# Score visits of three chunks, unit 2 normed on VectorE, and the first pair loaded by head, in a fused cosine attention and cosine-gated MLP

## The chip, the cores and the metric

The kernel runs on one core of a Trainium2 chip. The metric is the device time of one execution in microseconds (us), as the median of five runs. Beside it stands one profiled execution, whose trace gives the times of all instructions. Engines are named as in the profile: PE (TensorE), PEld (its weight loads), DVE (VectorE), ACT (ScalarE), POOL (GpSimd) and SP (SyncE, which here only issues transfers).

## The reference

Attention over 8 batches, 12 heads, 448 positions and 64 channels, with q and k normed to length 1, and then an MLP on the joined heads (3584 rows of 768):

```
q_n = q / (norm(q) + 1e-6);  k_n = k / (norm(k) + 1e-6)
attn = softmax(q_n @ k_n.T / tau)            # tau = 0.1
x = (attn @ v), heads side by side           # 3584 x 768
h = x @ w_in                                 # 768 x 2048
out = (h * cos(h)) @ w_out                   # 2048 x 768
```

Inputs and output are float32.

## The kernel before

**Units and pairs.** A batch has 12 heads: two units of six heads, each of three pairs. Pairs are numbered g = 0 to 47, units u = 0 to 15; batch b holds pairs 6b to 6b + 5. A sequence of 448 is laid out as 112 partitions by 4.

**What a pair needs.** `load` brings k and q of a pair or of a whole unit into `raw` (two buffers, by the parity of u), `load_v` brings v. The norm of a pair is a chain: `square` (on ACT, DVE or POOL, by `PLAN` for units 0 and 1, mostly POOL afterwards), `reduce` (a DVE reduction), `rnorm` (ACT: logarithm, then exponential of minus a half of it, L708 and L711; one call for a whole unit from unit 2 on) and `scale` (POOL, or DVE for pair 0). `transposes` turns the scaled pair into `qkT`: by PE and a DVE copy (L745, L753) for g < `BYPE` = 9, by a DMA transpose issued from SP afterwards (L734). `copy_v` casts v into `va`.

**Scores and attention.** A pair's scores come in four chunks of 112 keys. `scores` makes a chunk for two heads at once, each in one half of PE's rows (L762), in bank SC1 or SC0 by turns, and an ACT exponential takes it out into `PX` (L767). `both` makes two chunks back to back: this document calls such a run of score matmuls a visit. `attend` multiplies a pair's `PX` with `va` into bank AV (32 small matmuls, L785), and DVE takes the reciprocal of the sums and the product (`rcp` L794, `xs` L795). `xs` is transposed into `xT`, by PE (`XP`, in bank AV, L809, for batch 0 and the last pair of each batch) or by a DMA transpose from SP (L801).

**The MLP.** `m1(b)` is the first product for a batch: 16 column blocks of six matmuls of 448 columns (96 in all, L826), two blocks to a bank, over three banks by turns (`TURN`: SC0, SC1, AV), each followed by ACT's sine with a shift (L840) and a DVE product into `gT` (L842). M1's blocks 0 to 7 use the first half of W1, 8 to 15 the second. The second product, M2, makes 128 rows by 384 columns in 16 matmuls (L877) into PO or PO2, and a DVE copy into `osb` (L884); outputs are issued from SP. M2 is the filling work: PE takes it while ACT makes exponentials.

**Tables.** ACT loads a table before the sines and another before the exponentials (1.28 us each, L618).

**The order.** The program is a list of operations with their dependences. A planner in the kernel (`arrange`, `play`, `rehearse`) plays the list with constants for the costs, several times with other margins (`TRIALS`), keeps one order for each engine, and `emit` writes it out with semaphore waits, so each engine's order is fixed when the kernel runs. PE's main stream is taken nearly in program order, M2 (stream B) wherever it fits; where the plan has holes, matmuls of zeros are put in (the fillers, L919). The order of POOL and SP matters because both also issue transfers: W1 (L908) and W2 (L914) are issued from POOL and cast on the way, all else from SP, but for the first unit's q, from ACT.

**Around the change.** The first six pairs are computed while the weights come in; `norms(2, 0)` stands before `m1(0)`, so ACT makes unit 2's logarithms before it loads the sine table. `pair(g)` is the body of the main loop: two visits, `attend(g - 1)` between them, loads and norms for later units. `points` puts `m1(b)` after pair 12 for b = 1 and after one pair more of the next batch for the others, and all of M2 of that batch is queued behind it.

Of the kernel before, what the change touches and what calls it, by code (L numbers as in the profile page):

```python
# [6 lines left out]
ACT = mybir.ActivationFunctionType  # L7
# [7 lines left out]
    "sq": ["AD", "A", "P", "P", "P", "P"],  # L15
# [4 lines left out]
DEBUG = 0  # L20
PACE, AHEAD = 0.97, 9.5
# [7 lines left out]
class Program:  # L29
# [11 lines left out]
    PATIENCE = 0.25  # L41
# [56 lines left out]
    def share(self, start, jobs, factor=1.0, first=1.2):  # L98
# [3 lines left out]
        came = {o.idx: start[o.idx] + first + (0.5 if e == "POOL" else -0.1) for e in jobs for o in jobs[e]}  # L102
# [69 lines left out]
    TRIALS = [(m, h, k) for m in ((0.0, 1.0), (0.3, 1.1), (0.8, 1.1)) for h in (0.1, 0.2) for k in (0.05, 0.2)]  # L172
# [3 lines left out]
    def arrange(self):  # L176
# [12 lines left out]
        for self.margin, self.hold, self.look in self.TRIALS:  # L189
            nominal, self.lands = first, {}  # L190
            for n in range(self.PASSES):
# [14 lines left out]
                if n:  # L206
                    spans = [self.rehearse(f, x) for f, x in self.STAGE]
                    if DEBUG:
                        print(self.margin, self.hold, self.look, n, "%.1f" % self.span, ["%.1f" % x for x in spans])
# [8 lines left out]
    def play(self):  # L218
# [45 lines left out]
        def pick():  # L264
# [4 lines left out]
            if groups and groups[0][0].free:  # L269
                for grp in groups[: self.WINDOW]:  # L270
# [3 lines left out]
                    if left[o.idx] == 0:  # L274
                        t = max(free["PE"], ready_at[o.idx])
                        if s is None or t < s - self.PATIENCE:
                            s, c = t, (t, o, grp)
                return c
            for grp in groups[:3]:
                t = when(grp)  # L280
                if t is not None and (s is None or switched(t, grp[0]) < s - self.PATIENCE):
                    s, c = switched(t, grp[0]), (t, grp[0], grp)
            if fill and left[fill[0].idx] == 0:
                o = fill[0]
                t = max(free["PE"], ready_at[o.idx])
# [16 lines left out]
        def transfer(upto):  # L302

            while clock[0] < upto:
# [10 lines left out]
                for h in run:  # L315
                    h[2] -= step * h[0].pkt / turn
                    if h[2] <= 1e-9:
                        o = queue[h[0].eng].pop(0)[0]
                        o.end = max(clock[0] + self.LAST, o.start + o.cost + 1.0)
                        if o.start > 5.0:  # L320
                            o.end += self.margin[0] + (self.margin[1] - 1.0) * (o.end - o.start)
# [8 lines left out]
        while todo or any(queue.values()):  # L330
# [23 lines left out]
            if e == "PE":  # L354
                if current:
                    current.pop(0)
                elif grp is fill:
                    fill.pop(0)
# [15 lines left out]
            if o.dma is not None:  # L374
                queue[e].append([o, o.start + (1.7 if e == "POOL" else 1.1), o.bulk + 0.02])
# [110 lines left out]
def bass_cosine_attention__then__act_gcu_kernel(  # L486
# [25 lines left out]
    BYPE = 9  # L512
# [5 lines left out]
    NO = 4  # L518
    DEFER = (2 * PB,)
# [58 lines left out]
    POv = PO.ap().bitcast(BF16)  # L578
    vav = [t.ap().rearrange("p (x d) -> p x d", d=DV) for t in va]
# [9 lines left out]
    XTv = AV.ap().bitcast(BF16)  # L589
# [48 lines left out]
    for i in range(2):  # L638
        pool(lambda e, i=i: e.memset(vav[i][:, :, D : D + 1], 1.0), (), [("va", i)], 0.15, label="ones")
# [7 lines left out]
    def load(u, p0, p1, apart=False):  # L647
        i = u % 2
        h = slice(2 * p0, 2 * p1)
        f = [lambda e, x=x, t=t: e.dma_start(  # L650
            rawv[i][:, h, NJ * x : NJ * x + NJ, :].rearrange("p h s d -> p h (s d)"), src(t, u, 2 * p0, 2 * (p1 - p0)))
            for x, t in enumerate((k, q))]
        for x in ((0,), (1,)) if apart else ((0, 1),):
            eng = "ACT" if u in HALF and x == (1,) else "SP"
            behind = quick[-1] if eng == "ACT" and quick else None if eng == "ACT" or not loads else loads[-1]
            dma(eng, [f[y] for y in x], (), [("raw", i, p, y) for p in range(p0, p1) for y in x],
                "raw%d_%d_%s%s" % (i, p0, x, eng), 0.95 * (p1 - p0) * len(x), "load u%d p%d" % (u, p0), behind, 0.068)
# [421 lines left out]
```

## Time and profile before

| | us |
|---|---|
| median of five runs | 433.33 (431.95 to 433.84) |
| the profiled execution | 431.95 |
| its span | 430.1 |
| PE busy, of the span | 418.3 |
| ACT busy | 264.5 |
| DVE busy | 212.7 |
| POOL busy | 192.9 |
| ACT exponentials (L767), 192 of 914 ns | 165.0 |
| M2 matmuls (L877) into PO, 816 | 148.6 |
| fillers (L919), 48 | 14.5 |

The span is the time from the first to the last instruction in the trace. "Busy" of PE counts the fillers, and the ends of matmuls are modelled, so the distance from one start to the next is the better measure of what a matmul costs. The last M1 starts near 377 us and 200 M2 matmuls follow it. The DMA engines are at or near 90% in the first 65 us, and moved 234 to 266 GB/s there. The granted TensorE clock is full throughout.

### The profile page before, as it was taken

What the parts mean: (1) busy time and instruction counts of PE and PEld (TensorE: products, weight loads), DVE (VectorE), ACT (ScalarE), POOL (GpSimd) and SP (SyncE); (2) the same over time, 40 slices, a digit from 0 to 9 for tenths busy, and PEclk for the clock granted to TensorE, in tenths of its full rate; (3) what the DMA queues carried; (4) which work ended last, traced back from release to release, by engine and by line L of the source; (5) the groups of instructions that cost most, each with busy time, mean ns of one, the idle gap of its engine ahead of it and who ended that gap; (6) DMA issues with size and microseconds to landing.
All of it is one profiled execution on the core that took longest, in us unless ns stands there. A gap on an engine that the chain in (4) does not pass through costs nothing.

```text
span 430.1 us, 8767 instructions
## 1 busy us (share of the span) xinstructions
PE 418.3 (97%) x3756; PEld 226.1 (53%) x3756; DVE 212.7 (49%) x297; ACT 264.5 (61%) x319; POOL 192.9 (45%) x118
## 2 busy tenths in 40 slices
PE   7889989999999999999999999999999999999996
PEld 3455545545555555555555545555555545555663
DVE  5776645464636366524853375425853343344221
ACT  3887386974777647774677638774777557734000
POOL 3995167823776556923496057913595000000000
PEclk9999999999999999999999999999999999999999
DMA  8999997898179595649657694649657102200322
GB/s 234 263 244 215 241 266 164 146 265 195 34 194 227 129 276 163 121 102 252 171 113 124 152 243 103 112 128 251 145 112 125 49 0 59 59 2 4 102 77 77
DMA packets 94631, 63.87 MB, mean 149 GB/s; under 512 B 55040, under 2 KB 89600, under 8 KB 94592
## 3 DMA queue, kind: packets, MB, share of 16 engines
q1 hardware_dynamic: 90064, 56.16, 56.0%
q0 software_dynamic: 3680, 6.29, 7.9%
q10 hardware_dynamic: 848, 0.86, 0.7%
q8 instruction: 30, 0.49, 0.5%
q14 instruction: 9, 0.07, 0.1%
HBM read 45.61 MB, written 11.01 MB: 132 GB/s over the span
## 4 chain that ended last, share of the span: by engine, by line
PE 82%; ACT 7%; POOL 3%; issue 2%; DVE 2%; DMA 2%; SPq 1%; POOLq 0%; ACTq 0%
PE PO L877 28%; PE SC L826 20%; PE AV L826 11%; PE AV L785 10%; PE SC L762 9%; ACT PX L767 5%; PE SC L877 2%; DMA raw<-in_q_dram 2%; POOL sq L693 2%; POOL qks L719 1%; PE AV L877 1%; DVE n L700 1%; DVE gT L842 1%; ACT cosb L840 0%; PE PO L745 0%
## 5 line engine op out<-in xcount | busy, mean ns | idle before, releaser
L767 ACT ACTIVATE PX<-SC 112x896 bf16<-112x896 f32 x192 | 165.0, 914 | 43.5 <-PE SC L762 43.1
L877 PE MATMUL PO<-W,gT 128*128 128x384 bf16 x816 | 148.6, 326 | 0.0
L693 POOL TENSOR_TENSOR sq<-raw 112x1024 bf16<-112x1024 f32 x42 | 79.4, 1908 | 97.9 <-DMA raw<-in_q_dram 97.9
L877 PEld LDWEIGHTS PO<-W,gT 128*128 128x128 bf16 x816 | 73.0, 97 | 56.8 <-issue 13.1
L719 POOL TENSOR_TENSOR qks<-raw,rn 112x1024 bf16<-112x1024 f32 x47 | 88.5, 1904 | 27.9 <-ACT rn L711 27.8
L826 PE MATMUL SC<-xT,W 128*128 128x448 bf16 x480 | 95.5, 352 | 0.2 <-DVE xT L813 0.2
L842 DVE TENSOR_TENSOR gT<-SC,cosb 128x896 bf16<-128x896 f32 x40 | 43.5, 1091 | 55.2 <-ACT cosb L840 54.8
L840 ACT ACTIVATE cosb<-SC,cst 128x896 f32<-128x896 f32 x40 | 40.2, 1007 | 48.6 <-PE SC L826 46.2
L826 PEld LDWEIGHTS SC<-xT,W 128*128 128x128 bf16 x480 | 46.6, 98 | 43.0 <-issue 0.6
L700 DVE TENSOR_REDUCE n<-sq 112x16 f32<-112x1024 bf16 (+1 forms) x49 | 58.0, 1190 | 13.0 <-POOL sq L693 8.2
L762 PE MATMUL SC<-qkT 64*128 64x448 bf16 x384 | 55.5, 355 | 4.2 <-ACT PX L767 2.2
L826 PE MATMUL AV<-xT,W 128*128 128x448 bf16 x288 | 58.7, 352 | 0.6
L785 PEld LDWEIGHTS AV<-va,PX 112*128 112x128 bf16 x1536 | 49.4, 97 | 15.6 <-issue 11.3
L785 PE MATMUL AV<-va,PX 112*128 112x65 bf16 x1536 | 54.8, 193 | 1.0 <-ACT PX L767 1.0
L884 DVE COPY osb<-PO 128x384 f32<-128x384 f32 x51 | 28.2, 553 | 39.3 <-PE PO L877 39.3
L840 ACT ACTIVATE cosb<-AV,cst 128x896 f32<-128x896 f32 x24 | 24.2, 1007 | 32.0 <-PE AV L826 31.9
L794 DVE RECIPROCAL rcp<-AV 112x8 f32<-112x8 f32 x48 | 9.9, 207 | 67.0 <-PE AV L785 67.0
L826 PEld LDWEIGHTS AV<-xT,W 128*128 128x128 bf16 x288 | 27.6, 98 | 28.1 <-issue 3.1
L842 DVE TENSOR_TENSOR gT<-AV,cosb 128x896 bf16<-128x896 f32 x24 | 26.2, 1090 | 18.7 <-ACT cosb L840 18.5
L795 DVE TENSOR_TENSOR xs<-AV,rcp 112x512 bf16<-112x512 f32 x48 | 33.2, 691 | 2.0
L762 PEld LDWEIGHTS SC<-qkT 64*128 64x128 bf16 x384 | 13.3, 94 | 36.7 <-ACT PX L767 17.4
L667 POOL CAST va<-vin 112x1536 bf16<-112x1536 f32 x14 | 20.5, 1466 | 10.1 <-DVE gT L842 5.8
(34 smaller groups left out, 122.9 us busy)
## 6 DMA issues: line engine op xcount, KB each, us to landing
vin<-in_v_dram SPq DMA_DIRECT2D x16, 672.0 KB, 10.2
raw<-in_k_dram SPq DMA_DIRECT2D x12, 672.0 KB, 8.1
raw<-in_q_dram SPq DMA_DIRECT2D x12, 672.0 KB, 10.0
W<-in_moe_w_in_dram POOLq DMA_DIRECT2D x2, 1536.0 KB, 14.4
W<-in_moe_w_out_dram POOLq DMA_DIRECT2D x4, 768.0 KB, 20.9
raw<-in_k_dram SPq DMA_DIRECT2D x12, 224.0 KB, 7.0
out_dram<-osb SPq DMA_DIRECT2D x7, 336.0 KB, 2.8
out_dram<-osb SPq DMA_DIRECT2D x8, 288.0 KB, 2.7
```

The lines of the kernel that those rows point to most:

```text
L693: pool(lambda e, x=x, y=y: e.tensor_tensor(y, x, x, ALU.mult), src_, dst, 0.1 + n * 1.78e-3, label="sq%d.%d" % (u, p))
L700: dve(lambda e, w=w: e.tensor_reduce(out=n2v[i][:, 2 * p : 2 * p + 2, w], in_=sqv[p][:, :, w, :], axis=mybir.AxisListType.X, op=ALU.add), ...
L719: f = lambda e, s0=s0, s1=s1: e.tensor_tensor(qksv[i][:, p, s0:s1, :, :].rearrange("p s h d -> p h s d"), rawv[i][:, h, s0:s1, :], bass.AP ...
L762: t = e.matmul(SCv[z][:, a, 0:S], qkT[k].ap()[r, NP * c : NP * c + 128], qkT[k].ap()[r, S : 2 * S], start=True, stop=True)
L767: act(lambda e: e.activation(PXv[j][:, c, 0 : 2 * S].rearrange("p (a s) -> p a s", a=2), SCv[z][0:NP, :, 0:S], ACT.Exp, scale=1.0 / TAU), ...
L785: t = e.matmul(AVv[:, a, DV * x : DV * x + n], PXv[j][:, c, k : k + 128], vav[i][:, NJ * (2 * p + a) + c, 0:n], start=(c == 0), stop=(c == ...
L795: dve(lambda e: e.tensor_tensor(xsv[y].rearrange("p x h d -> p h x d"), AXv[:, :, :, 0:D], bass.AP(rcp[y], 0, [[NS, NP], [NJ, 2], [1, NJ], ...
L826: t = e.matmul(ph[:, a, 0:S], W1v[:, c, 128 * n : 128 * n + 128], xTv[b % 2][:, c, :], start=(c == 0), stop=(c == NKC - 1))
L840: act(lambda e, ph=ph, cz=cz: e.activation(cosv[cz], ph[:, :, 0:S], ACT.Sin, bias=cst.ap()[:, 0:1], scale=1.0), names(gi) + ["cst0"], [("c ...
L842: dve(lambda e, ph=ph, cz=cz, gi=gi: e.tensor_tensor(gTv[:, 2 * gi : 2 * gi + 2, S * (b % 2) : S * (b % 2) + S], ph[:, :, 0:S], cosv[cz], ...
L877: r = e.matmul(po[:, 0:HW], gTv[:, y, col : col + 128], W2v[:, y, HW * hf : HW * hf + HW], start=(y == 0), stop=(y == NF - 1))
L884: dve(lambda e, po=po, o=o, hf=hf: e.tensor_copy(osb[o].ap()[:, HW * hf : HW * hf + HW], po[:, 0:HW]), keys, [("osb", o, hf)], HW, label=" ...
```

## The change

1. **Visits of three.** For g >= `G3` = 12, `visit` makes three chunks, which take the banks AV, SC0, SC1; the 12 chunks of three pairs make four visits (`ahead`, `visit`, `attend`, `values`, with `project` for M1 after the second visit). Pairs 6 to 11 keep visits of two. XP and, for pairs 8 to 11, the PE transposes change banks.
2. **Unit 2.** Its loads wait until the first half of W1 has landed; its norm is done pair by pair, on DVE, by an integer guess and three Newton steps: 11 small operations for each pair. All its squares are POOL's. `BYPE` is 12: pairs 9 to 11 are transposed by PE as well.
3. **The first pair** is loaded, squared and reduced a head at a time.
4. **W1 and W2.** Both halves of W1 are issued from POOL one after the other behind the first POOL square (u0 p2); W2 is issued behind the last scale of unit 1. Unit 1's first square moves from POOL to ACT.
5. **M2** is dealt out evenly (`SPREAD`, `KEEP`): 144 matmuls of it are left after the last M1.
6. **v** is cast in thirds on DVE for units 0 and 1, and `attend` is split finer in the first six pairs. **Planner:** other margins, a larger delay for transfers from POOL, and other rules for choosing M2.

```
-    "sq": ["AD", "A", "P", "P", "P", "P"],
+    "sq": ["AD", "A", "P", "A", "P", "P"],
...
-    TRIALS = [(m, h, k) for m in ((0.0, 1.0), (0.3, 1.1), (0.8, 1.1)) for h in (0.1, 0.2) for k in (0.05, 0.2)]
+    TRIALS = [(m, h, k, p) for m in ((0.3, 1.1), (0.7, 1.1)) for h in (0.2, 0.32) for k in (0.4, 0.5) for p in (0.15, 0.25)]
...
-                queue[e].append([o, o.start + (1.7 if e == "POOL" else 1.1), o.bulk + 0.02])
+                queue[e].append([o, o.start + (5.0 if e == "POOL" else 1.1), o.bulk + 0.02])
...
-    BYPE = 9
+    BYPE = 12
...
+        if u == 0 and p0 == 0 and BYHEAD:
+            for a in range(2):
+                for x, t in enumerate((k, q)):
+                    eng, past = ("SP", loads) if x == 0 else ("ACT", quick)
+                    dma(eng, [lambda e, x=x, t=t, a=a: e.dma_start(
+                        rawv[i][:, a : a + 1, NJ * x : NJ * x + NJ, :].rearrange("p h s d -> p h (s d)"), src(t, u, a, 1))],
+                        (), [("raw", i, 0, x, a)], "raw%s%d" % (eng, a), 0.45, "load u0 p0", past[-1] if past else None, 0.063)
+                    past.append(P.ops[-1])
+            return
...
+        if u in NEWTON:
+            m, t, y = n2[i].ap()[:, w], lnn[i].ap()[:, w], rn[i].ap()[:, w]
...
+            def small(f, reads, writes):
+                dve(f, reads, writes, n, label="rn%d.%d" % (u, p0))
+
+            small(lambda e: e.tensor_scalar(m, m, 1e-12, None, ALU.add), km, km)
+            small(lambda e: e.tensor_scalar(y.bitcast(I32), m.bitcast(I32), -0.5, 1597463007.0, ALU.mult, ALU.add), km, ky)
+            for x in range(STEPS):
+                small(lambda e: e.scalar_tensor_tensor(t, y, -0.5, m, ALU.mult, ALU.mult), km + ky, kt)
+                small(lambda e: e.tensor_tensor(t, t, y, ALU.mult), kt + ky, kt)
+                small(lambda e: e.scalar_tensor_tensor(y, t, 1.5, y, ALU.add, ALU.mult), kt + ky, ky)
+            return
...
+        if g >= PB + UP - 1:
+            views, keys = (AVt, AVt), ("AV", "AV")
...
     def scores(g, c):
-        j, k, z = g % 2, g % UH, (c + 1) % 2
+        j, k, q = g % 2, g % UH, NJ * g + c
+        name, bank = PHs[1 + (c + 1) % 2 if g < G3 else q % 3]
...
+        keys, view = ["PO"], POv
+        if g >= 2 * PB - 1:
+            keys, view = [(["PO"], POv), ([("TP", 0), ("TP", 1)], TPv)][nhalf[0] % 2]
+            nhalf[0] += 1
...
+        if g >= 2 * PB - 1:
+            m2_emit(max(0, len(m2_queue) - KEEP[g // PB - 1]))
...
+    def visit(g, n):
+        q = NJ * g + 3 * n
+        for x in range(q, q + 3):
+            scores(x // NJ, x % NJ)
...
+    def project(b, g):
+        first = len(P.ops)
+        m1(b)
...
+        m2_add(b)
+        m2_emit(SPREAD[b])
...
     load_w1(0)
-    after(P.ops[-1], find("load v u0"))
     load_w1(1)
...
+    P.order_only(find("sq0.2"), find("W1.0"))
+    P.order_only(find(BEHIND), find("W1.1"))
+    last_scale = find(LASTW)
     for p in range(UP):
         load(2, p, p + 1)
+        if BEFORE2:
+            after(P.ops[-1], find(BEFORE2))
     load_w2(0)
+    P.order_only(last_scale, P.ops[-1])
     load_w2(1)
-    norms(2, 0)
...
     m1(0, 2, NKC - 1)
     copy_v(2)
     P.free = False
     banks[0] = [("PO", PO.ap()), ("PO2", PO2.ap())]
+    for p in range(UP):
+        norms(2, p, p + 1)
+        if p < UP - 1:
+            transposes(PB + p)
     m2_add(0)
...
+    m2_emit(SPREAD[0])
+    for g in range(PB, G3):
+        ahead(g)
+        grouped(both, g, 0)
+        if g > PB:
+            attend(g - 1)
...
+    for g in range(G3, NG, 3):
+        for n in range(4):
+            if n < 3:
+                ahead(g + n)
+            grouped(visit, g, n)
+            if n < 3 and g + n > PB:
+                attend(g + n - 1)
+            if n == 0:
+                values(g)
+            if g % PB == 0 and g > PB and n == (AT if g > 2 * PB else AT1):
+                project(g // PB - 1, g)
     attend(NG - 1)
```

## The prediction

> **What bounds the kernel now.** I read the shares per slice first, then the table by stage, then the timeline of one steady pair and of the first microseconds, and last the waits of the head.
>
> ```profile
> 9.50:36.50 27.00, 23.46 (x323) 12.94 (x324) 20.51 (x29) 22.92 (x35) 24.44 (x17) 1.00 1.12 248
> 36.50:58.00 21.50, 21.39 (x136) 11.40 (x135) 11.79 (x15) 10.06 (x12) 7.56 (x5) 1.00 1.14 244
> 58.00:90.00 32.00, 30.61 (x344) 16.52 (x341) 17.49 (x27) 26.84 (x35) 23.72 (x14) 1.00 0.88 184
> 239.28:287.04 47.76, 47.66 (x441) 25.55 (x440) 24.79 (x34) 32.13 (x39) 25.32 (x14) 1.00 0.71 153
> ```
>
> Columns: the stretch, its length, busy us of PE, weight load, DVE, ACT and POOL, then clock, DMA share and GB/s. From about 140 us on, PE has no idle time (47.66 of 47.76 us for one batch) while ACT has 15 us spare and DVE 23. In the head PE's 23.46 is swollen by idle fillers (48 in all); there ACT (22.92 of 27) and POOL (24.44 of 27) are nearly full, and the DMA engines are. So a steady gain must take time off PE itself; a gain in the head must shorten the ACT and POOL chain.
>
> ```profile
> 143.36 4.54 PE SC L826 x24
> 394.17 11.70 PE PO L877 x72
> ```
>
> These pieces of the chain of waits give PE's pitch: 4.54/24 = 0.189 us for 448 columns, 11.70/72 = 0.1625 for 384.
>
> ```profile
> 115.90 0.55 PE L762 MATMUL SC<-qkT 64*128 64x448 bf16 x4
> 116.30 1.73 ACT L767 ACTIVATE PX<-SC 112x896 bf16<-112x896 f32 x2 [0.69 <-PE SC L762]
> 116.38 1.14 PE L785 MATMUL AV<-va,PX 112*128 112x65 bf16 x32
> 117.36 0.81 PE L877 MATMUL PO<-W,gT 128*128 128x384 bf16 x4
> 117.56 0.21 DVE L794 RECIPROCAL rcp<-AV 112x8 f32<-112x8 f32 x1 [3.35 <-PE AV L785]
> 117.80 0.69 DVE L795 TENSOR_TENSOR xs<-AV,rcp 112x512 bf16<-112x512 f32 x1
> 118.11 0.55 PE L762 MATMUL SC<-qkT 64*128 64x448 bf16 x4
> ```
>
> One score visit, in starts: two chunks (two row halves at once) from 115.90 to 116.38 take 0.48, of which 2 x 0.189 is work: 0.10 is lost on leaving. Four M2 matmuls take 117.36 to 118.11, 0.75 for 0.65 of work: 0.10 lost on entering. A visit costs 0.20 us beside its work. Within it the second chunk starts 0.20 after the first (a narrower look at the same visit), 0.01 over the pitch.
>
> **Part 1: three chunks to a visit, from pair 12 on.** 36 pairs make 72 visits now and 48 after: 24 x 0.20 = 4.8 saved, less 24 more chunk-to-chunk steps of 0.01: **-4.6 us**. Bounds: -5.0, and -3.6 if a third chunk drains as much as a quarter of a switch. All of it is on the path, since PE is never idle there.
>
> The price is the third bank. AV now also takes a score chunk, so attend waits for that chunk's exp, and the next visit waits for xs. By the rows: exp begins 0.40 after the visit (115.90 to 116.30) and its first chunk takes 0.92, so AV is free at 1.32; the order gives PE 3 x 0.189 + 0.10 + four M2 (0.65), 1.32 with switches: no margin. Attend to xs done is 118.49 - 116.38 = 2.11; the order gives 0.96 + eight M2 (1.30) + 0.10 = 2.36: margin 0.25, if DVE is free. An osb copy (0.55) or a norm reduction (1.22) standing ahead of rcp breaks it. DVE's order puts the osb copies behind xs mostly, and two reductions in the stretch with no attend. Between 0 and 0.2 us for each of 36 attends, 0 to 7 in all; the nearer row is the margin of 0.25 that still holds with DVE half idle, so I take 0.04 each: **+1.5**.
>
> **Part 2: the head.** The first pair is loaded a head at a time, so each reduction starts when its half is there. Now q's square runs at 4.63, two reductions 5.36 to 6.65, rn at 7.26; split, the first head is reduced before the second lands, and about 0.65 (one reduction) comes off the first exp. That gain is caught at pair 1: both W1 issues (1.02 and 0.88) now stand on POOL ahead of the scales of pairs 1 and 2, where one stood; 0.9 later on POOL, against 0.65 earlier before it. In return POOL loses a square (1.9, given to ACT at 1.04) and the W2 issues that stood ahead of the last scale (1.5): 3.4 earlier by the last pair.
>
> ```profile
> POOL sq L693 <- DMA raw<-in_q_dram: 6.5, 1, 6.5
> ACT PX L767 <- PE SC L762: 5.0, 5, 1.7
> ```
>
> ACT sat 5.0 us in five waits for scores; 1.53 of them (before pair 1) stay, of the 1.8 after 23 us I count most back, less ACT's extra square. M1 of batch 0 starts at 36.34 now, **35.5** after (bounds 33.8, if only the 1.53 and the extra square are left of the 5.0, to 36.8, if W1's second half, now beside the unit-1 loads in a DMA system at 1.12 share, delays those).
>
> Unit 2's loads now wait on SP for W1's first half; behind them wait unit 3's loads, V, outputs and transposes. In the trace W issues land after 11.9 to 25.4 us. That moves unit 2's squares from 30 to about 36 us, under M1, where POOL has 12 idle us.
>
> **Part 3: unit 2's norms on DVE.** ln, rn (0.58) and a square (1.08) leave ACT ahead of the sine table. Eleven tiny operations for each of three pairs come to DVE. No such row exists; xs costs 0.69 for 512 elements and a 1024 reduction 1.21, so the constant is about 0.15, and 16 elements make 0.17, plus 0.04 between dependent operations (rcp ends 117.77, xs starts 117.80): 33 x 0.21 = 7.0 us. The bounds are the 0.06 us memset row (3.3 with gaps) and rcp's 0.21 (8.2).
>
> [...]
>
> DVE under M1 then holds 8 x 1.09 (gT) + 3 x 1.22 + 7.0 = 19.4 us against PE's 96 x 0.189 = 18.2, and eleven of them stand ahead of the last two gT. M1 has only three banks, so PE waits.
>
> ```profile
> 7.26 1.29 DVE L719 TENSOR_TENSOR qks<-raw,rn 112x512 bf16<-112x512 f32 x2 [0.62 <-ACT rn L711]
> 7.91 2.40 POOL L693 TENSOR_TENSOR sq<-raw 112x1024 bf16<-112x1024 f32 x1 [6.46 <-DMA raw<-in_q_dram]
> ```
>
> A POOL square that began beside a DVE multiply of two SBUF inputs took 2.40 instead of 1.90. So 27 of the 33 operations may in turn wait out a POOL operation (1.9 us): while pair 6 is scaled, pair 7's chain stands, then pair 8's. By the row that is up to 0.7 + 1.9 = 2.6 more.
>
> [...]
>
> The stall of PE in M1 is between 0 and 1.2 + 2.6 = 3.8; I take 2.0. M1 ends at 35.5 + 18.2 + 2.0 = 55.7, against 56.25 now (with three transposes in it that now follow).
>
> **From there to M1 of batch 1** the work is 96 M2 (15.6), 30 chunks (5.7), 7 attends (6.7), six transposes (6 x 0.39 = 2.3; three of them took the DMA path), one more 0.2, 14 visits' worth of switches (2.8): 33.3. Now 26.9 of work and 3.0 of switches take 33.9, so 4.0 are stalls, most of them the wait at 58.7 to 61.9 for first exps. Transposes and M2 fill part of that; pair 6's copy now stands behind late gT copies. I take 1.5 (0.5 to 4). M1 of batch 1 starts at 90.5, against 90.14, with two chunks, an attend and a visit (1.5) more done: **-1.1**.
>
> **Covered.** The V copies in thirds (6 x 0.69 against 2 x 1.74) lie in DVE's idle 6 us of the head. M2 moved from the tail (200 matmuls after the last M1, now 144) is the same PE work; its cover is lost only if attention were ACT-bound, and ACT has 32 of 48 us. The changed planner constants only move the order counted here.
>
> **Sum.** -1.1 - 4.6 + 1.5 = -4.2: span 430.1 to 425.9. The profiled execution took 431.95, 1.85 over its span, and the median 433.33 is 1.38 over that: 425.9 + 1.85 + 1.38 = **429.1**.
>
> **Rivals.**
> (a) The AV bank takes it back. Decides from (4.2 + 1.5)/36 = 0.16 us for each attend. If one attend in four meets a reduction of 1.22, that is 11.0: 430.1 - 1.1 - 4.6 + 11.0 = 435.4, time **438.6**, slower. For: no margin by the rows. Against: DVE half idle.
> (b) The Newton chains cost their bounds: 1.8 more in M1, 2.5 more behind: 425.9 + 4.3 = 430.2, time **433.4**, no change. For: the 2.40 us square. Against: POOL waits for the same chain, so they can't collide for long.
> (c) The early part goes well: start at 33.8, no stall in M1, 0.5 behind, no AV waits: -1.7 - 2.0 - 1.0 - 1.5 = -6.2: time **422.9**. For: 4 idle ACT us. Against: pair 1's scale is later.
> (d) The visits don't do what they say: the third chunk drains like a new visit, saving nothing: 429.1 + 4.6 = **433.7**. Against: the 0.01 step.
>
> **Chances.** Forecast 0.48, (a) 0.13, (b) 0.14, (c) 0.21, (d) 0.04. Own range of the forecast 426.5 to 431.8; to hold 8 in 10, from 424 (half of (c)) to 433.6 (most of (b); (a) is left out). A measurement tells 0.3%, 1.3 us, from no change: faster than 432.0 holds the forecast, (c) and a third of (b): 0.74; same 0.11; slower, (a) and the rest: 0.15.
>
> **What would show it.** Score rows of six matmuls, steady batches near 48.8 us at 112 M2 matmuls (now 47.76 at 100); PE waiting for xs or an AV exp by under 0.1 a pair; DVE rows of 0.17; M1 of batch 1 near 90. Wrong if steady PE idle time passes 1 us a batch, or that start lies past 93.

## The result and the profile after

| | before | after |
|---|---|---|
| median, us | 433.61 (431.85 to 437.87, 45 runs) | 434.49 (433.13 to 437.16, 24 runs) |
| profiled execution, us | 431.95 | 436.41 |
| its span, us | 430.1 | 434.6 |
| M1 of batch 0 starts at | 36.34 | 37.30 |
| M1 of batch 1 starts at | 90.14 | 94.43 |

The changed kernel is slightly slower: ratio 1.0022, 95% interval 1.0007 to 1.0037. Forecast was 429.1 with a span of 425.9. The two profiled executions lie on different sides of their medians (before 1.7 below, after 1.9 above), so their spans differ by 4.5 us where the medians differ by 0.9. The table by stage of the kernel after, with the columns of the one shown of before:

```profile
9.50:36.50 27.00, 23.20 (x292) 13.49 (x290) 17.66 (x30) 23.18 (x36) 19.81 (x14) 0.94 1.12 231
12.00:15.00 3.00, 0.58 (x4) 0.19 (x3) 2.82 (x4) 1.89 (x4) 2.99 (x3) 1.00 1.13 262
15.00:20.00 5.00, 4.58 (x56) 3.29 (x56) 2.68 (x5) 3.74 (x7) 4.48 (x4) 0.66 1.13 240
36.50:58.00 21.50, 19.95 (x142) 10.87 (x139) 18.62 (x42) 7.63 (x9) 9.48 (x5) 1.00 1.13 243
58.00:90.00 32.00, 29.92 (x355) 16.91 (x354) 19.93 (x34) 26.80 (x34) 24.74 (x14) 1.00 0.71 154
245.45:294.97 49.52, 49.34 (x457) 26.91 (x454) 24.89 (x34) 31.83 (x39) 25.34 (x14) 1.00 0.64 148
```

Three things differ. In the head PE did 0.58 us of work in 12 to 15 us, and after that its granted clock (third number from the right) was 0.66 over 5 us. In M1 of batch 0 DVE is busy 18.62 of 21.50 us (11.79 before), and PE has 1.55 us of idle time in it, where it had 0.1 before (busy 19.95 against 21.39). A stretch in which PE stands and waits is called a hole below. And a steady batch takes 49.52 us: it holds 112 M2 matmuls where the batch of before, 47.76, held 100. Twelve matmuls at 0.1625 are 1.95, so before would take 49.71 for the same work. The gain is 0.19 us a batch; 0.8 had been expected from four visits fewer at 0.20.

The pitches did not change. The chain of waits of the kernel after has

```profile
196.06 4.56 PE SC L883 x24
...
407.81 7.80 PE PO L931 x48
```

0.190 us and 0.1625 us a matmul. With them PE's lost time of a stage is its length less its matmuls at their pitch; for a steady batch it was 2.86 before (12 visits) and is 2.67 after (8 visits).

**Where the 0.8 went.** The timeline after, over two visits of three and the attends behind them, only the lines that matter (`...` stands for lines left out):

```profile
228.08 0.36 PE L811 MATMUL AV<-qkT 64*128 64x448 bf16 x2
...
228.48 0.92 ACT L816 ACTIVATE PX<-AV 112x896 bf16<-112x896 f32 x1 [0.72 <-PE AV L811]
...
228.75 0.82 PE L931 MATMUL PO<-W,gT 128*128 128x384 bf16 x4
...
229.45 1.02 PEld L834 LDWEIGHTS AV<-va,PX 112*128 112x128 bf16 x32 [0.27 <-ACT PX L816]
...
230.43 1.47 PE L931 MATMUL PO<-W,gT 128*128 128x384 bf16 x8
...
231.83 0.36 PE L811 MATMUL AV<-qkT 64*128 64x448 bf16 x2
...
232.50 1.47 PE L931 MATMUL PO<-W,gT 128*128 128x384 bf16 x8
...
233.05 1.72 ACT L816 ACTIVATE PX<-SC 112x896 bf16<-112x896 f32 x2
234.01 1.02 PEld L834 LDWEIGHTS AV<-va,PX 112*128 112x128 bf16 x32 [0.42 <-ACT PX L816]
```

A visit of three costs what was forecast: 228.08 to 228.75 is 0.67 for 0.57 of work. But attend now starts where an exponential ends. Four M2 matmuls from 228.75 are done at 229.40, attend starts at 229.45, as the exponential of the chunk in AV ends (228.48 + 0.92). The next attend needs the second chunk of its visit too, in SC0. Eight M2 from 232.50 are done at 233.80, attend starts at 234.01. A steady batch has four waits of 0.05 and two of 0.21, 0.62 in all, 0.10 for each attend. The xs product never made PE wait by more than 0.1 there.

**The head.** The chain of waits, then ACT and PE in the same stretch:

```profile
2.16 7.59 DMA raw<-in_q_dram
...
9.89 0.98 POOL sq L720
...
11.73 1.85 POOL W L964 x2
...
13.58 1.93 POOL qks L761
```

```profile
9.30 0.92 ACT L816 ACTIVATE PX<-SC 112x896 bf16<-112x896 f32 x1 [0.49 <-PE SC L811]
...
13.07 0.31 ACT L750 ACTIVATE lnn<-n,cst 112x16 f32<-112x16 f32 x1 [2.41 <-DVE n L726]
...
13.54 2.51 ACT L816 ACTIVATE PX<-SC 112x896 bf16<-112x896 f32 x3
```

```profile
10.57 1.50 PE L975 MATMUL PO<-zt 128*128 128x448 bf16 x7
14.49 0.36 PE L811 MATMUL SC<-qkT 64*128 64x448 bf16 x2 [2.42 <-ACT PX L816]
...
15.56 0.81 PE L793 MATMUL PO<-ident,qks 112*128 112x112 bf16 x8 [0.41 <-POOL qks L761]
16.16 1.53 PE L834 MATMUL AV<-va,PX 112*128 112x65 bf16 x24
```

The first exponential comes 0.57 earlier than before (9.30 against 9.87), near the 0.65 forecast, but not in the way that was forecast: the second half of q had landed at 4.24, before the first reduction began at 4.61, so no head was reduced ahead of the other's landing. And pair 2's q load, now the fourth on ACT's queue and not the third, lands at 9.75; before, POOL's square of pair 2 began at 7.91. Pair 2's logarithm stands on ACT ahead of pair 0's last three exponentials and waits 2.41 us for that square's sum; PE waits 2.42. The transposes that followed took 0.81 us for eight, where before they took 0.57: that is the clock, which by the table in stretches of half a microsecond stood at 0.50 from 15.7 to 19.1.

**M1 of batch 0.** DVE and POOL:

```profile
48.88 1.02 DVE L747 TENSOR_TENSOR lnn<-lnn,rn 112x16 f32<-112x16 f32 x1
...
51.24 0.88 DVE L747 TENSOR_TENSOR lnn<-lnn,rn 112x16 f32<-112x16 f32 x1
...
53.88 1.08 DVE L899 TENSOR_TENSOR gT<-AV,cosb 128x896 bf16<-128x896 f32 x1
...
55.58 1.89 DVE L747 TENSOR_TENSOR lnn<-lnn,rn 112x16 f32<-112x16 f32 x1
```

```profile
47.98 1.89 POOL L720 TENSOR_TENSOR sq<-raw 112x1024 bf16<-112x1024 f32 x1 [2.90 <-DMA raw<-in_q_dram]
50.19 1.90 POOL L761 TENSOR_TENSOR qks<-raw,rn 112x1024 bf16<-112x1024 f32 x1 [0.32 <-DVE lnn L746]
55.54 1.90 POOL L761 TENSOR_TENSOR qks<-raw,rn 112x1024 bf16<-112x1024 f32 x1 [3.44 <-DVE lnn L746]
```

```profile
55.10 2.43 PE L883 MATMUL AV<-xT,W 128*128 128x448 bf16 x12 [1.55 <-DVE lnn L746]
...
60.31 0.57 PE L793 MATMUL PO<-ident,qks 112*128 112x112 bf16 x8 [1.73 <-DVE qkT L801]
```

A Newton operation takes 0.17, but three that began beside a POOL operation ended with it: 48.88 + 1.02 is 49.90, the square ended at 49.87; 51.24 + 0.88 and 50.19 + 1.90 are 52.12 and 52.09; 55.58 + 1.89 and 55.54 + 1.90 are 57.47 and 57.44. Unit 2's squares wait for loads held back behind W1 until 38.20, 43.18 and 47.98. So the chains stand on DVE ahead of the gT product that frees bank AV (53.88), and PE waits 1.55 for it, then 1.73 for pair 6's copy.

### The profile page after: what moved, and what is told of

It is laid out like the page before. It is cut to its first block, busy times and chain, and to the rows that moved or that the text cites. A ratio compares the mean times of both kernels' runs of the same rounds, so it can differ in the third digit from the quotient of the medians.

```text
span 434.6 us, 8854 instructions
## 1 busy us (share of the span) xinstructions
PE 418.4 (96%) x3775; PEld 229.7 (53%) x3775; DVE 222.5 (51%) x338; ACT 262.3 (60%) x318; POOL 192.3 (44%) x118
## 4 chain that ended last, share of the span: by engine, by line
PE 73%; POOL 8%; DMA 6%; ACT 5%; DVE 3%; SPq 3%; issue 1%; ACTq 0%; POOLq 0%
PE PO L931 26%; PE SC L883 17%; PE AV L883 10%; PE AV L834 9%; POOL qks L761 5%; PE SC L811 5%; DMA raw<-in_q_dram 4%; ACT PX L816 4%; PE AV L811 3%; SPq L780 2%; POOL sq L720 2%; DMA vin<-in_v_dram 2%; PE AV L931 1%; PE SC L931 1%; DVE lnn L747 1%
## 5 line engine op out<-in xcount | busy, mean ns | idle before, releaser
L931 PE MATMUL PO<-W,gT 128*128 128x384 bf16 x832 | 152.2, 327 | 0.7 <-DVE osb L940 0.7
L816 ACT ACTIVATE PX<-SC 112x896 bf16<-112x896 f32 x144 | 122.8, 918 | 5.9 <-PE SC L811 5.9
L931 PEld LDWEIGHTS PO<-W,gT 128*128 128x128 bf16 x832 | 74.2, 98 | 64.1 <-issue 20.1
L816 ACT ACTIVATE PX<-AV 112x896 bf16<-112x896 f32 x48 | 44.0, 917 | 47.9 <-PE AV L811 47.9
L834 PEld LDWEIGHTS AV<-va,PX 112*128 112x128 bf16 x1536 | 50.4, 98 | 14.9 <-ACT PX L816 11.7
L834 PE MATMUL AV<-va,PX 112*128 112x65 bf16 x1536 | 56.8, 194 | 0.6
L811 PE MATMUL SC<-qkT 64*128 64x448 bf16 x288 | 42.1, 354 | 3.9 <-ACT PX L816 2.8
```

The source lines that it names most:

```text
L811: t = e.matmul(bank[:, a, 0:S], qkT[k].ap()[r, NP * c : NP * c + 128], qkT[k].ap()[r, S : 2 * S], start=True, stop=True)
L816: act(lambda e: e.activation(PXv[j][:, c, 0 : 2 * S].rearrange("p (a s) -> p a s", a=2), bank[0:NP, :, 0:S], ACT.Exp, scale=1.0 / TAU), [n ...
L834: t = e.matmul(AVv[:, a, DV * x : DV * x + n], PXv[j][:, c, k : k + 128], vav[i][:, NJ * (2 * p + a) + c, 0:n], start=(c == 0), stop=(c == ...
L931: r = e.matmul(po[:, 0:HW], gTv[:, y, col : col + 128], W2v[:, y, HW * hf : HW * hf + HW], start=(y == 0), stop=(y == NF - 1))
```

## The experiments

Theory A: the visits' saving is real, and attend's wait for the exponential in AV gives most of it back; the rest of the loss comes from the head (loads by head) and from DVE's order in and behind M1 of batch 0. Rivals: the visits save nothing; W1's two issues on POOL make the head late; the chains' operations themselves, not their place, make the holes; the planner's constants do it. The last one has one test only (`soon0`, one constant); no run puts the other constants back.

**Both kernels again, and visits of two.** `c_before` is the kernel before unchanged, `c_after` the changed one. `two` keeps all of the change but the visits of three (with it, M1 of a batch stands after a whole pair again, and other numbers of M2 matmuls fall into a batch):

```
-    G3 = 12
+    G3 = NG
...
-    for g in range(PB, G3):
+    for g in range(PB, NG):
```

> The kernel before, unchanged, for a second profile of it. If the two profiles of before and after were ordinary ones, this one has its M1 of batch 0 start within 1 us of 36.3, M1 of batch 1 near 90.1 and steady batches of 47.76. If the head varies from run to run (its transfers fill the DMA engines), the start of M1 of batch 0 moves by 1 us or more, and part of the 4.5 us between the two profiled spans is no effect of the change.

> The changed kernel, unchanged. Ratio to before about 1.002. Theory 'head varies': M1 of batch 0 starts anywhere in 35 to 37.5 and the span shifts with it, while the steady batches stay at 49.53 with 112 M2 matmuls. Theory 'the change delays the head': M1 of batch 0 starts at 37.3 again and POOL's first square at 9.9.

> The changed kernel with visits of two chunks for all pairs, nothing else undone. Theory A (the 24 visits fewer save 0.20 us each, but attend now waits 0.05 to 0.21 us for the exponential of a chunk of its own visit, 0.6 us a batch): a steady batch of 112 M2 goes from 49.53 to 49.7, the whole by 1 us or less. My prediction's term (saving 4.6, waits 1.5) would make it 3 us slower than the changed kernel. Rival (three banks cost more than they bring): up to 2 us faster.

`c_before` took 435.86 (one run, span 434.0): its M1 of batch 1 started at 91.45, and PE had a hole of 1.46 at 161.4 to 162.8 that the first profile had not. So these two executions of the kernel before differ by 3.9 us of span, and such a hole is in one and not in the other. `c_after` took 435.85, ratio 1.0029 (1.0004 to 1.0054), with steady batches of 49.52 to 49.53 again. `two` took 438.07, ratio 1.0104 (1.0059 to 1.0149), 2.2 us above `c_after`. Its undisturbed steady batch (116 M2) lost 2.68, as much as with visits of three; one hole of 2.03 at 142.6, for a DMA transpose of xs, shows in it. What makes it slower over its runs is not settled by its one profile, so `two` alone does not show what the visits are worth.

**Half an exponential in AV.** From pair 24 on `halfexp` leaves out half of each exponential in bank AV, so its output is not the reference's; it is there to time the wait.

```
+        ha = 1 if name == "AV" and g >= 2 * G3 else 2
-        act(lambda e: e.activation(PXv[j][:, c, 0 : 2 * S]..., bank[0:NP, :, 0:S],
+        act(lambda e: e.activation(PXv[j][:, c, 0 : ha * S]..., bank[0:NP, 0:ha, 0:S],
```

> The changed kernel, same order on every engine, but from pair 24 on the exponential of each chunk that lies in bank AV takes one head of the two (448 columns instead of 896); the other head's part of PX keeps older values, so half of these chunks is left out. Theory V (attend waits for the exponential that empties bank AV, 0.62 us a steady batch of the changed kernel, as two waits of 0.21 and four of 0.05): that exponential ends 0.4 earlier, the four waits of 0.05 and one part of the two of 0.21 go, a steady batch at 112 M2 matmuls takes 48.9 to 49.1 instead of 49.53, PE's lost time per batch 2.1 to 2.3 instead of 2.67, the whole kernel 2 to 3 us (0.5 to 0.7%) below the changed kernel. Rival S (the third chunk of a visit or the new order costs PE itself, not the wait for the exponential): the batch stays at 49.5.

The table by stage of this kernel (one steady batch), and one cycle of its timeline:

```profile
242.88:291.76 48.88, 48.78 (x458) 27.40 (x455) 24.90 (x34) 28.85 (x39) 25.34 (x14) 1.00 0.62 150
```

```profile
226.30 0.54 ACT L817 ACTIVATE PX<-AV 112x448 bf16<-112x448 f32 x1 [1.04 <-PE AV L811]
...
226.57 0.82 PE L932 MATMUL PO<-W,gT 128*128 128x384 bf16 x4
...
227.23 1.13 PE L835 MATMUL AV<-va,PX 112*128 112x65 bf16 x32
```

With the same order, attend follows its four M2 at once (226.57 + 0.65 is 227.22), a batch takes 48.88 and PE loses 2.02 in it: 0.84 less than before. Median 432.41, ratio 0.9952 (0.9929 to 0.9976), against 1.0022 for the changed kernel. 0.84 is the forecast saving of the visits; with the longer exponential 0.65 of it is taken back in each batch.

**The head.** `nohead` loads the first pair whole (`BYHEAD = False`), `w1late` puts W1's second half behind pair 1's scale (`P.order_only(find("scale1.0"), find("W1.1"))`), `soon0` sets `SOON = 0.0`.

> The changed kernel with its first pair loaded whole, as in the kernel before (part 3 of the change undone); everything else stays. Theory H (the head starts late because each pair-0 load is cut in four and the loads behind them, those of pair 2 and of q above all, land later, so that POOL's first square waits to 9.89 instead of 7.91, and everything on POOL behind it): that square again near 8, pair 1's first exponential near 16.5 instead of 18.2, M1 of batch 0 near 36.0 instead of 37.3, ratio to the kernel before 0.3% lower than that of the changed kernel (1.0022): about 0.999. Rival W (the late head comes from the two W1 issues that stand on POOL ahead of pair 1's scale, not from the loads): the first square may move but pair 1's scale stays near 13 and M1 of batch 0 near 37, ratio 1.002.

> The changed kernel with W1's second half issued from POOL behind the scale of pair 1 instead of behind the first square; everything else stays. Rival W: pair 1's scale begins 0.9 to 1.0 us earlier (12.6 instead of 13.6), its first exponential near 17.2, M1 of batch 0 near 36.4, ratio to the kernel before about 1.000. Theory H: the first square still waits for its load to 9.9, POOL then has the same work a little later, ACT's row of exponentials is only shifted, M1 of batch 0 within 0.3 of 37.3 and the ratio near 1.002.

> The changed kernel with the one planner constant that pulls the logarithms of the first two units forward (SOON) set from -4 to 0: on ACT the exponentials of pair 0's chunks now stand ahead of pair 2's logarithm. Nothing is left out. Theory A (in the changed kernel pair 2's logarithm, which waits for POOL's late square, stands ahead of pair 0's last three exponentials; ACT stalls 2.41 us, PE 2.42, and PE's granted clock then falls to 0.66 in 15 to 20 us): no PE hole over 1 us before 16 us, clock 1.00 in 15 to 20 us, M1 of batch 0 starts at 36.0 to 36.5 instead of 37.3, ratio to the kernel before 0.999. Rival L (the hole is POOL's and the loads', the order on ACT only decides where it is seen): the hole appears before pair 1's scores instead, M1 of batch 0 at 37 or later, ratio 1.002.

| | first POOL square | pair 1's scale | PE hole before 16.2 us | half clock | M1 of batch 0 | ratio |
|---|---|---|---|---|---|---|
| after | 9.89 | 13.58 | 2.42 | 15.7 to 19.1 | 37.30 | 1.0022 |
| nohead | 8.68 | 12.39 | 0.29 | none | 35.52 | 0.9981 (0.9956 to 1.0007) |
| w1late | 9.37 | 12.24 | 2.01 | 14.7 to 18.1 | 37.41 | 1.0024 (0.9994 to 1.0053) |
| soon0 | 10.45 | 14.15 | 2.62 | 17.8 to 24.6 | 38.94 | 1.0029 (1.0005 to 1.0054) |

Theory H holds: with whole loads the square starts 1.2 earlier and M1 of batch 0 at 35.52. The square's start varies from one execution to the next (9.15 in `c_after`), but over all profiles with the changed kernel's planner the two groups do not meet: 9.15 to 10.61 in the ten with loads by head, 8.02 to 8.78 in the eight with whole loads. Rival W falls: in `w1late` pair 1's scale did begin 1.3 earlier (0.5 of it because the square did) and M1 no earlier, because ACT still waits for pair 2's sum. In `soon0` ACT's order is the other one, and rival L is what was seen:

```profile
16.13 0.57 PE L793 MATMUL PO<-ident,qks 112*128 112x112 bf16 x8 [2.62 <-POOL qks L761]
```

The hole moves to pair 1's transposes. The late load makes it, not the order that shows it.

**The Newton chains.** `steps1` does one step (norms of unit 2 good to 0.2%), `stt` writes the multiply as a scalar-tensor-tensor, `unit2act` puts unit 2 back on ACT with early loads, `early2` only lets its loads go early (`BEFORE2 = ""`).

```
-    NEWTON, STEPS = (2,), 3
+    NEWTON, STEPS = (2,), 1
...
-                small(lambda e: e.tensor_tensor(t, t, y, ALU.mult), kt + ky, kt)
+                small(lambda e: e.scalar_tensor_tensor(t, t, 1.0, y, ALU.mult, ALU.mult), kt + ky, kt)
...
-    NEWTON, STEPS = (2,), 3
+    NEWTON, STEPS = (), 3
```

> One Newton step in place of three, so the norm of unit 2 is only good to 0.2%: 15 small operations on DVE instead of 33. Theory A (the chain under M1 of batch 0 holds gT and the copy of pair 6 back): PE's 1.55 us hole in M1 and the 1.73 us wait before pair 7's transposes go, first exponential of pair 6 near 58.5 instead of 61.4 (with M1 starting at 37.3), M1 of batch 1 2 to 3 us earlier; time 1.5 to 3 us less than the changed kernel's. Rival (ACT or the loads of unit 2 hold the stage anyway, squares come 3 to 5 us apart behind their loads): under 0.5 us less.

> The changed kernel with the one multiply of each Newton step that has two operands of equal kind (TENSOR_TENSOR, 9 of the 33 operations) written as a scalar-tensor-tensor with 1.0, so that all operations of the chains are of the forms that took 0.17 us throughout. Theory P (in the changed kernel three of the nine TENSOR_TENSOR waited out a POOL operation, 1.02, 0.88 and 1.89 us, and no other form of the chain did): those rows are gone, every chain operation takes about 0.17, the two PE holes of 1.55 and 1.73 us in M1 of batch 0 and behind it shrink to under 1 together, M1 of batch 0 is 18.7 long instead of 20.1, M1 of batch 1 2 us earlier (92.4), ratio to the kernel before 0.998. Rival (any DVE operation with two inputs waits for POOL then, or the holes come from unit 2's late squares): the waits move to the new rows or the holes stay, and the ratio stays at 1.002.

> The changed kernel with unit 2 as in the kernel before: its loads no longer wait behind W1's first half, one square of its three on ACT, its norms by logarithm and exponential on ACT before the sine table; everything else stays. Theory N (the Newton chains and the late squares of unit 2 cost PE the holes of M1 of batch 0 and of the stage behind it, 8.3 us lost in 37.3 to 94.4 against 7.4 before with the same visits and more to do): M1 of batch 0 starts 1 to 1.5 us later (a square of 1.08, a logarithm and an exponential more on ACT), but no port wait of 0.9 to 1.9 in it, its length back to about 18.5, pair 6's first exponential near 59.5, M1 of batch 1 near 92.5, span 432.5, ratio to the kernel before 0.998. Rival (the chains only fill idle DVE time, and the holes come from the three extra transposes and copies): M1 of batch 1 later than 94, ratio 1.004 or more.

> The changed kernel with unit 2's loads no longer held back behind W1's first half (they stand on SP where the kernel before had them); the Newton chains on DVE stay. Nothing is left out. Theory T (the chains are not too long but too late: unit 2's squares wait for their loads to 38.2, 43.2 and 48.0, so the chains stand among the last gT products of M1 of batch 0, and PE waits 1.5 to 3.7 for bank AV at 55 us): squares near 31 to 36, no PE hole over 0.8 between 50 and 61 us, M1 of batch 1 at 91.5 to 92.5 instead of 94.4, ratio to the kernel before 0.997 to 0.999. Rival K (the chains' 33 operations and the waits beside POOL's scales make the hole wherever they stand): a hole over 1.5 before M1's last block again, M1 of batch 1 past 93.5, ratio 1.001 or more.

| | holes of PE, 42 to 64 us | M1 of batch 0 to M1 of batch 1 | ratio |
|---|---|---|---|
| after | 1.55, 1.73 | 57.13 | 1.0022 |
| c_after | 0.94, 0.70, 1.73 | 58.95 | 1.0029 |
| steps1 | 1.61 | 55.54 | 1.0003 (0.9982 to 1.0024) |
| stt | 1.84, 1.73 | 57.41 | 1.0003 (0.9981 to 1.0025) |
| unit2act | 0.92 | 57.04, with 12 M2 fewer | 1.0026 (1.0000 to 1.0051) |
| early2 | 2.23, 1.35 | 58.71, with 4 M2 fewer | 1.0066 (1.0033 to 1.0098) |

In these profiles the stretch of `steps1` is 1.6 us shorter than that of the changed kernel. That this is the worth of two steps is not shown: M1 of batch 0 began later in `steps1` (38.12), and `soon0`, with all three steps and M1 at 38.94, took 54.46 for the stretch with 4 M2 fewer (0.65 us), as little as `steps1`. Nor do the ratios of `steps1` and the changed kernel lie apart by more than their intervals. Theory P falls; the timeline of `stt` has the same waits in the other form:

```profile
51.32 0.88 DVE L747 SCALAR_TENSOR_TENSOR lnn<-lnn,rn 112x16 f32<-112x16 f32 x1
...
55.65 1.89 DVE L747 SCALAR_TENSOR_TENSOR lnn<-lnn,rn 112x16 f32<-112x16 f32 x1
```

Theory T falls as well. With early loads the chains are early, and stand ahead of the first gT products instead:

```profile
42.80 1.89 DVE L747 TENSOR_TENSOR lnn<-lnn,rn 112x16 f32<-112x16 f32 x1
44.73 1.82 DVE L748 SCALAR_TENSOR_TENSOR rn<-lnn,rn 112x16 f32<-112x16 f32 x1
...
47.09 2.08 DVE L899 TENSOR_TENSOR gT<-SC,cosb 128x896 bf16<-128x896 f32 x2
```

```profile
48.32 6.38 PE L883 MATMUL SC<-xT,W 128*128 128x448 bf16 x24 [2.23 <-DVE gT L899]
```

PE's 24 matmuls then took 6.38 instead of 4.70: the clock fell again, to 0.50 from 49.5 to 52.9. `unit2act` had no such waits in M1 (its expectation calls them port waits; the rows show that the two operations end together, not what joins them), but theory N's gain did not come: its M1 began at 37.87, behind the late head and ACT's added work, and M1 of batch 1 at 94.91.

**Parts together.** `nh_s1`, `nh_u2`, `nh_early` are `nohead` with one step, with unit 2 as before, and with early loads; the two with `b9` also leave pairs 9 to 11 to the DMA (`BYPE = 9`).

> The changed kernel with the first pair loaded whole and one Newton step instead of three for unit 2 (its norms then good to 0.2%). Theory: the two gains add, since they lie in different stretches: M1 of batch 0 at 35.5 (as with the first pair loaded whole alone) and the stretch to M1 of batch 1 about 2 shorter than with three steps, start of M1 of batch 1 near 91.5, span 430.5, ratio to the kernel before 0.994 to 0.996. Rival D (what PE loses in one place is a fall of the granted clock after a hole, which then moves to the next hole): a stretch of 5 us with a clock below 0.8 shows up after M1 of batch 0 again and the ratio is 0.998 or more.

> The changed kernel with the first pair loaded whole and unit 2 as in the kernel before (early loads, one square on ACT, logarithm and exponential on ACT before the sine table). What is left of the change then is the visits, the transposes by PE, the W issues, the spread of M2 and the planner. Theory: M1 of batch 0 starts at 36.0 (one square, one logarithm and one exponential more on ACT than with the first pair loaded whole alone, 35.5), is 18.4 long without a hole, M1 of batch 1 at 92.5; ratio to the kernel before 0.997. Rival (unit 2 on ACT was no better with the first pair loaded by head, ratio 1.0026, because the transposes and copies of pairs 6 and 7 behind M1 make the holes): M1 of batch 1 past 94, ratio 1.000 or more.

> The changed kernel with the first pair loaded whole and unit 2's loads early; three Newton steps, visits, transposes and planner as in the change. Theory T with the head put right: M1 of batch 0 at 35.5 to 36, M1 of batch 1 at 90.5, clock 1.00 throughout, ratio to the kernel before 0.993 to 0.996. Rival D (a granted clock that falls after a PE hole takes back what is won): a fall shows and the ratio is 0.998 or more.

> First pair loaded whole, unit 2 as in the kernel before, and pairs 9 to 11 transposed by DMA again instead of by PE (BYPE 9); visits, W issues and planner as in the change. The six transposes on PE were 2.3 us of its work, three of them 1.2: theory: PE's work before M1 of batch 1 is 1.2 less than with PE transposes, its clock stays 1.00, M1 of batch 1 at 90.3 (91.46 with PE transposes), ratio to the kernel before 0.998 (1.0016 with them). Rival: the DMA transposes land late (in the kernel before pair 8's or 9's scores waited 0.6 for one), and the ratio stays above 1.000.

> First pair loaded whole, unit 2's loads early with the Newton chains, and pairs 9 to 11 transposed by DMA: the parts that the runs so far speak against are undone, the visits and the Newton norms stay. Theory: both gains add to about 0.992 to 0.995 of the kernel before. Rival: DVE's chains and the DMA transposes meet in the stage behind M1 of batch 0, ratio 0.998 or more, as with the other combinations.

Ratios: `nh_s1` 0.9984 (0.9962 to 1.0006), `nh_early` 0.9985 (0.9961 to 1.0010), `nh_u2` 1.0016 (0.9993 to 1.0038), `nh_u2_b9` 1.0049 (1.0024 to 1.0073), `nh_early_b9` 1.0037 (1.0014 to 1.0060). M1 of batch 0 began at 35.42 to 36.97 in all five. The rest of the expectations failed: nothing was added to `nohead`'s gain. `nh_early` has a PE hole of 2.75 before 46.4 and the clock at 0.50 from 46.9 to 50.3. `nh_u2` had a clock of 1.00 throughout and M1 of batch 1 at 91.46, but with 84 M2 done by then instead of 96: twelve at 0.1625, 1.95 us, come later. With transposes by DMA again both kernels were 0.3 to 0.5% slower than without, though PE had 1.2 us less to do; one wait for such a transpose (0.77 before 87.1) shows in `nh_early_b9`. That profile has two more holes that `nh_early` had not, 1.98 before 111.4 for a gT product and 1.00 before 146.3 for a transpose of xs; what makes them is open. The profiled execution of `nh_s1` lay 4.8 us above its median, so its hole of 3.69 is not read as typical.

**The order on DVE.** `gt2` is `nohead` with two order edges: pair 7's chain behind the sixth gT product, pair 8's behind the eighth. `gt1` has one: pair 8's reduction behind the eighth.

```
+    for p, x in ((1, 5), (2, 7)):
+        P.order_only(find("g0.%d" % x), [o for o in P.ops if o.label == "rn2.%d" % p][0])
     m2_add(0)
```

> First pair loaded whole, and pair 8's reduction and Newton chain ordered on DVE behind the last gT product of M1 of batch 0 (one order edge); everything else as in the change. Theory Q (the hole before M1's last block is one of DVE's queue: bank AV's gT product stands behind pair 8's reduction and the chains, which wait for squares that end at 43 to 50; pair 8 is not needed before 75 us): no PE hole over 0.8 between 42 and 62 us, clock 1.00 there, M1 of batch 0 18.5 to 19 long, M1 of batch 1 at 91 to 92 (95.6 with the first pair loaded whole alone), ratio to the kernel before 0.992 to 0.995. Rival K (whatever stands there, the chains beside POOL's operations make a hole somewhere): a hole over 1 us between 42 and 62, ratio 0.997 or more.

> First pair loaded whole, pair 7's chain ordered on DVE behind the sixth gT product of M1 of batch 0 and pair 8's chain behind the eighth; reductions where the planner puts them. Theory Q: as for the kernel with pair 8 alone moved, M1's blocks wait for nothing but the two reductions, holes under 0.8 between 42 and 57; pair 7's transposes come up to 1 us later, M1 of batch 1 at 91 to 92.5, ratio 0.992 to 0.996. Rival K: a hole over 1 us there, ratio 0.997 or more.

`gt2` took 432.35 (431.16 to 434.09, 12 runs), ratio 0.9965 (0.9947 to 0.9982): faster than both kernels. How much of that the two edges give beside the whole load is not settled by the medians: the interval of `nohead`, 0.9956 to 1.0007, overlaps this one. The profile shows the holes that they take away. PE in M1 of batch 0, and the table by stage:

```profile
43.09 4.70 PE L883 MATMUL SC<-xT,W 128*128 128x448 bf16 x24 [0.32 <-DVE gT L899]
...
52.51 2.43 PE L883 MATMUL AV<-xT,W 128*128 128x448 bf16 x12 [0.18 <-DVE n L743]
```

```profile
35.59:54.77 19.18, 18.68 (x106) 9.44 (x103) 15.95 (x35) 6.95 (x7) 7.74 (x5) 1.00 1.14 240
54.77:91.92 37.15, 35.30 (x433) 20.42 (x432) 24.26 (x44) 30.06 (x38) 26.96 (x16) 1.00 0.74 180
```

M1 of batch 0 lasts 19.18 (20.07 after), its holes are 0.32 and 0.18, the clock is 1.00, and M1 of batch 1 starts at 91.92 with 96 M2 done. One hole of 1.38 is left at 63.4, for pair 8's scale. `gt1`, with the planner's other choices, went the other way: 441.9, ratio 1.0184 (1.0163 to 1.0204).

```profile
66.38 0.93 PE L793 MATMUL AV<-ident,qks 112*128 112x112 bf16 x8 [4.85 <-POOL qks L761]
```

```profile
60.65 1.82 DVE L744 TENSOR_SCALAR rn<-n 112x16 int32<-112x16 int32 x1
```

In M1 a hole of 2.73 stayed (before 54.3). Then pair 8's chain, last on DVE, met two POOL squares of unit 3 (58.69 to 62.43), pair 8's scale began at 64.43, and PE stood 4.85 us; the clock was at 0.50 for 10.2 us, from 63.6 on. Theory Q holds for `gt2` and failed for `gt1`: an order edge that moves one operation also moves what PE then waits for.

## Why the prediction was wrong

It forecast a span of 425.9; 434.6 was measured. The steps, in its own order:

- **What bounds the kernel**, PE's pitch and the 0.20 us of a visit: right. So is Part 1's saving: 24 visits by 0.20 is 0.8 a batch, and 0.84 was measured where attend hardly waits. (The sign "near 48.8" for a steady batch did not hold the prediction's own 0.04 for each attend: 47.76 + 1.95 - 0.77 + 0.24 is 49.2.)
- **The price of the AV bank, +1.5, failed in size.** The prediction wrote "no margin" for the exponential (1.32 against 1.32) and then priced attend by the other margin, the 0.25 of xs, which held. The wait that ends last was the first one, and it overlooked that every third attend needs the second chunk of its visit as well. Measured: 0.65 a batch, 0.11 for each attend, 3.9 us for 36, inside its bounds of 0 to 7. The order places no other work of PE there. Of rival (a) only the mechanism with the reduction was seen, twice and outside the steady batches (rcp at 142.05 and at 177.57 behind a reduction of 1.22, holes of 0.75 and 0.41).
- **The head, 35.5, failed**, beyond its bound of 36.8: 37.30 and 37.52. The step that failed is "about 0.65 comes off the first exp", which gave the gain and costed the loads behind it at nothing. Two loads cut in four put pair 2's q load 0.44 later on ACT's queue; it landed at 9.75 (9.01 in `c_after`, 8.54 with whole loads), and POOL and ACT both stood behind it. Why it can land later by more than 0.44 no run shows. The price of the W1 issues was right, but ACT did not wait for them. With the loads whole again M1 starts at 35.52, the forecast value (35.36 to 36.88 in the other runs with whole loads and the Newton norms): nothing there speaks against the rest of Part 2.
- **Part 3** was right in its parts: 0.17 us an operation, 3.3 us of waits beside POOL in three rows (2.6 allowed for), M1 20.07 long (20.2 forecast). What failed is when the chains come: unit 2's squares were put at "about 36", and began at 38.20, 43.18 and 47.98, so the second and third chain stood at the end of M1 and behind it; and rival (b)'s "can't collide for long" did not hold, with a single wait of 1.89. Early loads alone do not mend it (`early2`). That a DVE operation may last as long as the POOL operation beside it was an estimate from one row, the square of 2.40; the ends above, equal within 0.03 us, show it for three operations.
- **M1's end to M1 of batch 1 failed in size:** 37.06 against 34.8; stalls of 3.8 where 1.5 was taken, inside the bounds. The 1.73 at 60.31 is pair 6's copy behind late gT products, which the prediction named and priced too low; the gT product at 58.64 stood behind pair 8's chain. In `gt2` that hole is gone.
- **Left out of the sum:** the two batches after it. PE lost 5.17 and 3.25 there against 2.67 in a steady one; 4.24 and 3.63 in `c_after`, 4.01 and 2.66 in `gt2` (about 3.8, with 14 visits, and 2.6 in the kernel before). The prediction took the steady visit for all 36 pairs. Of the 3.1 us over steady batches, 1.8 are three holes behind norm reductions on DVE: the two of rcp, and one of 0.65 at 140.15 for an osb copy.

So the span went +1.8 (head), -0.1 (M1), +2.3 (to M1 of batch 1), +2.4 (AV bank) and +2.4 (mostly the batches after): 425.9 + 8.8 = 434.7. Rivals (c) and (d) did not occur; (b), 433.4, comes nearest to what was seen, since the stretch behind M1 cost 2.3 more where it allowed 2.5; but M1 itself was not longer than forecast, and the head and the AV bank cost as much again. That (d), 433.7, lies nearer still to the measured 434.49 is chance, for the visits did save what was forecast. The median lies 5.4 above the forecast, not 8.7, since the forecast added 1.4 for an execution below the median and this profile was one above it.

What stays open: which of the planner's many moved operations put reductions ahead of rcp and osb there and cost the rest of the batches up to 190 us, what its other constants do, what the Newton steps are worth, and why `two` is slower over its runs than its profile shows.

## What to carry to other kernels

Where a bank gets one more user, write down for each user the wait that ends last, with no credit from the waits that have margin, and count whether the filling work is there. On an engine whose order the program fixes, an operation whose input comes late belongs behind those that free a bank for PE, unless PE then waits for that operation itself, as in `gt1`; here one load made whole again and two order edges turned 1.0022 into 0.9965. When loads are cut finer, look at who stands behind them on the queue: pair 2's q load landed at 9.75 here, and at 8.54 with whole loads.

## What was not expected of the hardware

The granted clock of TensorE fell to 0.50 after many of PE's holes (in `gt1` within one), and stayed there for 3.4 us (15.7 to 19.1 after; 61.3 to 64.7 in `nohead`), 6.8 us (14.6 to 21.4 in `c_after`) or 10.2 us (63.6 to 73.9 in `gt1`). The rows of `nohead`, table by stage and timeline:

```profile
61.00:65.00 4.00, 4.00 (x22) 1.95 (x22) 1.38 (x3) 3.07 (x4) 4.00 (x3) 0.57 0.89 223
```

```profile
59.92 0.57 PE L793 MATMUL PO<-ident,qks 112*128 112x112 bf16 x8 [1.74 <-DVE qkT L801]
...
60.91 2.41 PE L931 MATMUL PO<-W,gT 128*128 128x384 bf16 x8
```

Eight M2 take 2.41 instead of 1.47. So `nohead` gained 1.8 us before M1 of batch 0 and lost some of it here. Such a fall came with holes of 1.66 (before 13.75 in `c_after`) to 4.85 us (`gt1`); others of the same lengths had none behind them: 1.55 and 1.73 behind each other in the changed kernel, 1.76 in the head of `halfexp`, 2.73 before 54.3 in `gt1`, and 3.28 before 56.9 in `w1late`. So the length of the hole alone does not decide, and what does is not shown.

One DVE operation with a single SBUF input lasted until POOL's end too: the TENSOR_SCALAR of 16 elements at 60.65 in `gt1` took 1.82 instead of 0.17 and ended at 62.47, within 0.04 of POOL's squares (62.43).
